# One kernel for clustered attention and two MoE layers: the planner of the MoE part may put rests and sums on GpSimd or VectorE, squares are formed without a rectified copy, and the last block's projections use other PSUM banks

## The chip, the core and the metric

The kernel runs on one core of a Trainium2 chip. TensorE multiplies matrices into PSUM, VectorE and ScalarE work on PSUM and SBUF, GpSimd on SBUF, and SyncE issues the DMAs. The metric is the device time of one execution in microseconds (us). A change is compared with the kernel before on the same chip.

## The reference

```python
def reference(**kwargs):
    attn_out = _attn_ref(**attn_kwargs)          # (2, 8, 768, 64): attention within 16 clusters
    x = attn_out.transpose(0, 2, 1, 3).reshape(B * S, H * D)      # 1536 tokens x 512
    x = _moe_ref(x=x, **moe_kwargs)
    return _moe2_ref(x=x, **moe2_kwargs)

def _moe_ref(x, w_gate, w_val, w_out, rms_g):    # 512 -> 1536 -> 512
    rms = np.sqrt(np.mean(x * x, axis=-1, keepdims=True) + 1e-06)
    xn = x / rms * rms_g
    g = xn @ w_gate
    silu = g * (1.0 / (1.0 + np.exp(-g)))
    return (silu * (xn @ w_val) @ w_out).astype(np.float32)

def _moe2_ref(x, w_in, w_out, s, b):             # 512 -> 2048 -> 512
    r = np.maximum(x @ w_in, 0.0)
    return ((s * (r * r) + b) @ w_out).astype(np.float32)
```

Inputs and outputs are float32 (some come as float64). The change touches the two MoE layers alone.

## The kernel before

Each operand of a matrix product is held as a high part (rounded to TensorE's fp32r format) and a low part, the **rest** (value minus high part). A product is three matmuls: high by high, high by rest, rest by high. So for each operand ScalarE writes the high part and GpSimd subtracts to get the rest: `split_h` (lines 1161 and 1164, tiles `gh` and `gl`) for the hidden values, `part_` (lines 1203 and 1205, tiles `xh`/`xl` and `eh`/`el`) for the inputs of the second layer, `split_w` and `add_pair` (tiles `wh`/`wl`) for the weights.

The 1536 tokens are four blocks `t` of 384 (`TB`), the 512 channels four chunks of 128. The first layer (`kind` 1) has 12 slices `f` of 128 hidden units, taken in pairs. For a slice and a block `unit1` makes gate and value products (12 matmuls each) in PSUM banks of the pool `ps_g` (tiles `pg`, tag "g", five banks); `proj` multiplies the hidden values of a pair with `w_out` and adds the result to `acc` in SBUF. Its products go to banks of the pool `ps_o` (tiles `po`, tag "o", three banks), and VectorE adds each to `acc`.

The second layer (`kind` 2) has 16 slices in eight pairs. `quad2` computes two slices for two blocks (blocks 2u and 2u+1) by seven block products instead of eight: products a, b, c, a again, d, e, d again, six matmuls each, joined by five additions on VectorE. That needs sums and differences of input blocks, the **forms** `t1` to `t4`, beside the blocks themselves (`11`, `21`, `22`), each split in high part and rest. `finish` then takes each of the four results through relu (ScalarE), square (VectorE, line 1343), scale and bias (ScalarE, line 1347) and `split_h`. The first product `a` is copied to SBUF by ScalarE (line 1334) before the same bank takes a further product.

The forms for u = 0 need the last result of the first layer (block 1 of its last pair of slices). `forms_last` makes them straight from the PSUM banks of that last projection: `proj` takes its chunks in the order 0, 2, 1, 3, VectorE adds the older sums to each in PSUM (line 1186), and after chunks 2 and 3 the form's differences follow (line 1280, and one on GpSimd, line 1293), each with high part and rest.

The order of instructions is not the order of the code. Each step is recorded with its engine, a duration, what it reads, what it writes and the buffers it takes; a planner, `Plan.run`, then sets them one by one in the queues of the engines. In the MoE part (`post`) the order on TensorE is that of the code (`strict`), and every other step has a due time from `due`, counted back from the TensorE step that needs it. The engine of each step is fixed. Each engine then runs its queue in order; a step that waits holds all behind it.

The main loop sets TensorE's order: after each `quad2` it calls `flush()`, which puts the projections that were held back:

```python
            else:
                if fs[0] == 0 and t != blocks[0]:
                    flush()
                quad2(fs, t, s)
                flush()
```

At the change of layers this gives: the quad u=1 of slices 0 and 1, the last projection of the first layer (block 1), the projections of blocks 2 and 3, the quad u=0, then the quad u=1 of slices 2 and 3.

Of the kernel before, what the change touches and what calls it, by code (L numbers as in the profile page):

```python
# [20 lines left out]
F32 = mybir.dt.float32  # L21
# [23 lines left out]
class Plan:  # L45
# [4 lines left out]
    def __init__(self, bufs, strict=()):  # L50
        self.ops, self.bufs, self.strict = [], bufs, strict
        self.last_w, self.readers, self.users = {}, {}, {}
# [30 lines left out]
    def due(self):  # L83


        ops, taken, after, t = self.ops, {}, {}, 0.0
        late = [1e9] * len(ops)
        for n, o in enumerate(ops):
            for d in {*o[3], *self.bufdeps(n, taken)}:
                if d != n:  # L90
                    after.setdefault(d, []).append(n)
            for tile in o[4]:
                taken.setdefault(tile[0], []).append(tile)
            if o[0] in self.strict:
                late[n], t = t, t + o[1]
        seen = set()

        def visit(n):
            if n not in seen:
                seen.add(n)  # L100
                for m in after.get(n, ()):
                    visit(m)
                    late[n] = min(late[n], late[m] - LATENCY[ops[n][0]] - ops[n][1] - 2.5 * bool(ops[n][6]))

        for n in range(len(ops) - 1, -1, -1):
            visit(n)
        self.ops = [(*o[:5], late[n], o[6]) for n, o in enumerate(ops)]

    def run(self):
        if self.strict:  # L110
            self.due()
# [10 lines left out]
        line = [n for n, o in enumerate(ops) if o[0] in self.strict][::-1]  # L122

        def start(n):
            if ops[n][0] in self.strict and n != line[-1]:
                return None
# [12 lines left out]
        while ready:  # L139
# [15 lines left out]
            if eng in self.strict:  # L155
                line.pop()
# [17 lines left out]

LATENCY = {"PE": .2, "ACT": .15, "DVE": .18, "POOL": .08, "SP": .65}
# [4 lines left out]
def attention_moe_moe2_kernel(  # L180
# [455 lines left out]
    def split_w(raw, to, j, ramp=None, at=None):  # L636
# [11 lines left out]
        stt(out=ui, in0=b, scalar=2.0 ** 31, in1=up_, op0=ALU.min, op1=ALU.subtract, reverse1=True)  # L648
        stt(out=ai, in0=low, scalar=5, in1=ui, op0=ALU.logical_shift_right, op1=ALU.bitwise_or)
# [340 lines left out]
    post = Plan({  # L990
# [3 lines left out]
    }, ("PE",))  # L994
# [10 lines left out]
    def then(eng, dur, fn, r, w, new=(), more=0.0):  # L1005
        add(eng, dur, fn, r=r, w=w, new=new, prio=now[0] + more)
# [443 lines left out]
```

## Time and profile before

| | us |
|---|---|
| median of 3 runs (811.73, 812.53, 816.11) | 812.53 |
| the profiled execution | 811.1 |
| span from its first to its last instruction | 809.4 |
| TensorE busy | 764.3 |
| VectorE, GpSimd, ScalarE busy | 572.0, 507.8, 483.2 |
| mean granted clock of TensorE, share of full | 0.992 |

The span is what the trace covers; the profiled time is 1.7 us more. The attention part takes the first 290 us or so: the first rest of the planned MoE part (line 1164) starts at 293.4 us. The products of the second layer start at 538.8 us and run to the end.

### The profile page before, as it was taken

What the parts mean: (1) busy time and instruction counts of PE and PEld (TensorE: products, weight loads), DVE (VectorE), ACT (ScalarE), POOL (GpSimd) and SP (SyncE); (2) the same over time, 40 slices, a digit from 0 to 9 for tenths busy, and PEclk for the clock granted to TensorE, in tenths of its full rate; (3) what the DMA queues carried; (4) which work ended last, traced back from release to release, by engine and by line L of the source; (5) the groups of instructions that cost most, each with busy time, mean ns of one, the idle gap of its engine ahead of it and who ended that gap; (6) DMA issues with size and microseconds to landing.
All of it is one profiled execution on the core that took longest, in us unless ns stands there. A gap on an engine that the chain in (4) does not pass through costs nothing.

```text
span 809.4 us, 14303 instructions
## 1 busy us (share of the span) xinstructions
PE 764.3 (94%) x5409; PEld 705.3 (87%) x5409; DVE 572.0 (71%) x933; ACT 483.2 (60%) x933; POOL 507.8 (63%) x464
## 2 busy tenths in 40 slices
PE   3899999799999899999999999997799999999998
PEld 1678877699998889999999999996788988998996
DVE  6898888988685767666646534446688788778855
ACT  5578789667758446555425333354676677667642
POOL 7599989968889335444423533698465664664632
PEclk9999999999999999999999999999899999999999
DMA  8476886254421014433311201100121212122004
GB/s 117 95 133 123 134 171 150 62 116 122 107 79 54 27 52 130 126 94 120 104 52 63 95 1 52 53 1 1 53 78 53 78 53 78 56 76 78 27 1 156
DMA packets 98821, 65.15 MB, mean 80 GB/s; under 512 B 64992, under 2 KB 89664, under 8 KB 98752
## 3 DMA queue, kind: packets, MB, share of 16 engines
q1 hardware_dynamic: 98752, 64.24, 31.6%
q8 instruction: 42, 0.69, 0.4%
q14 instruction: 27, 0.22, 0.1%
HBM read 48.45 MB, written 3.15 MB: 64 GB/s over the span
## 4 chain that ended last, share of the span: by engine, by line
PE 81%; DVE 10%; POOL 4%; ACT 3%; issue 2%; DMA 1%; DVEq 0%; POOLq 0%; ACTq 0%
PE pg L661 24%; PE po L675 16%; PE pg L1311 14%; PE po L673 10%; PE mps L450 4%; PE pv L521 3%; PE sps L481 3%; PE sps L482 2%; DVE mt L458 2%; POOL al L498 2%; PE pv L511 2%; PE pg L673 1%; DVE xn L575 1%; ACT a L487 1%; PE asps L397 1%
## 5 line engine op out<-in xcount | busy, mean ns | idle before, releaser
L1164 POOL TENSOR_TENSOR gl<-hv,gh 128x384 fp32r<-128x384 f32 x104 | 117.7, 1138 | 174.5 <-ACT gh L1161 174.4
L498 POOL TENSOR_TENSOR al<-a,ah 128x768 f16<-128x768 f32 x80 | 135.9, 1718 | 16.1 <-ACT ah L494 15.3
L661 PE MATMUL pg<-xh,wh 128*128 128x384 f32 x384 | 129.4, 337 | 2.5 <-DVE xl L591 1.4
L661 PE MATMUL pg<-xh,wl 128*128 128x384 f32 x384 | 128.5, 335 | 0.0
L661 PE MATMUL pg<-xl,wh 128*128 128x384 f32 x384 | 128.4, 334 | 0.0
L683 DVE TENSOR_TENSOR acc<-po,acc 128x512 f32<-128x512 f32 (+1 forms) x156 | 95.2, 624 | 41.9 <-PE po L673 21.7
L655 POOL TENSOR_TENSOR wl<-wa,wh 128x512 fp32r<-128x512 f32 x58 | 76.8, 1330 | 58.4 <-ACT wh L652 52.6
L487 ACT ACTIVATE a<-sps 128x384 f32<-128x384 f32 x192 | 86.0, 488 | 29.3 <-PE sps L482 27.4
L458 DVE TENSOR_REDUCE mt<-mps 128x1 fp32r<-128x768 f32 x96 | 90.1, 946 | 14.0 <-PE mps L450 13.0
L675 PE MATMUL po<-wh,gh 128*128 128x512 f32 x192 | 75.0, 391 | 0.6 <-DVE acc L683 0.6
L675 PE MATMUL po<-wh,gl 128*128 128x512 f32 x192 | 75.2, 392 | 0.0
L675 PE MATMUL po<-wl,gh 128*128 128x512 f32 x192 | 75.1, 391 | 0.0
L661 PEld LDWEIGHTS pg<-xh,wh 128*128 128x128 f32 x384 | 72.1, 188 | 3.5 <-DVE xl L591 1.7
L481 PE MATMUL sps<-q 128*128 128x384 f32 x192 | 70.5, 367 | 3.5 <-DMA q<-mT 1.2
L1161 ACT ACTIVATE gh<-hv 128x384 fp32r<-128x384 f32 x104 | 52.4, 516 | 33.8 <-DVE hv L1152 32.7
L661 PEld LDWEIGHTS pg<-xl,wh 128*128 128x128 f32 x384 | 72.1, 188 | 0.0
L661 PEld LDWEIGHTS pg<-xh,wl 128*128 128x128 f32 x384 | 72.1, 188 | 0.0
L482 PE MATMUL sps<-q 128*128 128x384 f32 x192 | 64.6, 337 | 0.0
L673 PE MATMUL po<-gh,wh 128*128 128x384 f32 x168 | 56.8, 338 | 5.5 <-DVE th L1280 4.5
L450 PE MATMUL mps<-q 127*128 127x384 f32 x192 | 56.3, 384 | 3.2 <-DVE mt L458 2.1
L673 PE MATMUL po<-gh,wl 128*128 128x384 f32 x168 | 56.5, 336 | 0.0
L673 PE MATMUL po<-gl,wh 128*128 128x384 f32 x168 | 56.5, 336 | 0.0
(187 smaller groups left out, 1985.3 us busy)
## 6 DMA issues: line engine op xcount, KB each, us to landing
raw<-in_moe_w_out_dram SPq DMA_DIRECT2D x30, 511.6 KB, 3.5
raw<-in_moe_w_in_dram SPq DMA_DIRECT2D x16, 510.5 KB
raw<-in_moe_w_gate_dram SPq DMA_DIRECT2D x14, 510.5 KB, 4.1
raw<-in_moe_w_val_dram SPq DMA_DIRECT2D x14, 510.5 KB, 4.2
q<-q SPq DMA_DIRECT2D x14, 384.0 KB
q<-q SPq DMA_DIRECT2D x28, 192.0 KB, 2.7
vr<-in_v_dram SPq DMA_DIRECT2D x8, 384.0 KB
out_dram<-acc SPq DMA_DIRECT2D x12, 256.0 KB, 2.0
```

Source lines behind the costliest of these rows:

```text
L450: nc.tensor.matmul(ps[:, e, 0:HALF], lhsT=x[0:127, 1, c * 128:c * 128 + 128], rhs=x[0:127, 2, e * HALF:(e + 1) * HALF], start=True, stop=T ...
L458: nc.vector.tensor_reduce(out=mt_of[i][:, c:c + 1], in_=m_t.pop((i, c))[:, :, 0:HALF], axis=AX.XY, op=ALU.max)
L481: nc.tensor.matmul(ps[:, 0:HALF], lhsT=x[:, 2, ks], rhs=x[:, 1, cs], start=True, stop=False)
L482: nc.tensor.matmul(ps[:, 0:HALF], lhsT=x[:, 3, ks], rhs=x[:, 0, cs], start=False, stop=True)
L487: act(out=a_t[i, c][:, e * HALF:(e + 1) * HALF], in_=s_t.pop((i, c, e))[:, 0:HALF], func=ACTF.Exp, scale=scale)
L498: nc.gpsimd.tensor_tensor(out=al, in0=a_t.pop((i, c)), in1=ah_t[i, c], op=ALU.subtract)
L661: nc.tensor.matmul(ps, lhsT=a[:, kk * 128:kk * 128 + 128], rhs=x[:, kk, :], start=(kk == m == 0), stop=(kk == KC - 1 and m == 2),)
L673: nc.tensor.matmul(ps, lhsT=a[:, cs], rhs=x, start=st[0], stop=st[1])
L675: nc.tensor.matmul(ps, lhsT=x[:, cs], rhs=a, start=st[0], stop=st[1])
L683: tt(out=ac, in0=ps, in1=ac, op=ALU.add)
L1164: gps(out=gl, in0=src(), in1=gh.bitcast(F32), op=ALU.subtract)
L1311: nc.tensor.matmul(B(x), lhsT=a[:, k_ * 128:k_ * 128 + 128], rhs=b[:, k_], start=(not more and k_ == m == 0), stop=(k_ == 1 and m == 2), s ...
```

## The change

The planner of the MoE part becomes a class of its own, `Post`. Some steps now have a second engine and a second duration (`alt`), and the planner gives a step to VectorE where it would end earlier there than on GpSimd by its own numbers. These are the rests `gl`, most rests of forms, some differences of forms, and the sums and rests of the weight pairs (`either`). The square of results `u2` and `u3` is one instruction that reads the value twice, `max(x, 0) * x`, without the relu on ScalarE ahead of it; that of `c22` keeps its relu and may be a multiplication on GpSimd; that of `c11` stays. The two integer steps on the weights are two steps of the planner instead of one. The last projection of the first layer takes its four banks from the "g" pool, and `forms_last` reads them there. In the first pair of slices of the second layer `flush(1)` holds one projection back (block 3), which then stands behind the quad u=0.

```diff
+class Post(Plan):
...
+    def run(self):
+        ops, late, xfer = self.ops, self.due(), 0.0
...
+                t = max([done[d] for d in (*deps, *old)], default=0.0)
+                at = max(t, free[eng])
+                by.setdefault(eng, []).append((at, late[n], n))
+                if n in self.alt:
+                    e2, d2 = self.alt[n]
+                    a2 = max(t, free[e2])
+                    if a2 + d2 + GAIN < at + dur:
+                        by.setdefault(e2, []).append((a2, late[n], n))
...
+GAIN = 0.0
...
-    post = Plan({
+    post = Post({
...
+    def either(dur, d2, fn, r, w, new=(), more=0.0):
+        post.alt[len(post.ops)] = ("DVE", d2)
+        add("POOL", dur, fn, r=r, w=w, new=new, prio=now[0] + more)
+
+    def two(eng):
+        return tt if eng == "DVE" else gps
...
-        add("DVE", 1.75, step, r=[raw, b], w=[key, ("wd", n)], prio=prio)
+        add("DVE", .72, step, r=[b], w=[key], prio=prio)
+        add("DVE", .97, step, r=[raw], w=[key, ("wd", n)], prio=prio)
...
-        def lo():
+        def lo(eng):
             gh, gl = hs_t[kind, f, t]
-            gps(out=gl, in0=src(), in1=gh.bitcast(F32), op=ALU.subtract)
+            two(eng)(out=gl, in0=src(), in1=gh.bitcast(F32), op=ALU.subtract)
         then("ACT", .52, hi, [key], [(*hg, "h")], [hg])
-        then("POOL", 1.04, lo, [key, (*hg, "h")], [(*hg, "l")])
+        either(1.08, .97, lo, [key, (*hg, "h")], [(*hg, "l")])
...
-            o = ("o", (kind, fs[0], t, c))
-            def mm(c=c, o=o):
-                new_bank(o, ps_o)
+            g_ = kind == 1 and last and t == last_t
+            o = ("g" if g_ else "o", (kind, fs[0], t, c))
+            def mm(c=c, o=o, at=None if g_ else ps_o):
+                new_bank(o, at)
...
+            def square2():
+                temp["th", n, u, x] = tp[p].tile([128, TB], F32, tag="th", name="th")
+                stt(out=temp["th", n, u, x], in0=src(), scalar=0.0, in1=src(), op0=ALU.max, op1=ALU.mult)
...
-            then("ACT", .5, relu, [sk], [tk], [tk])
-            then("DVE", .56, square, [sk], [tk])
+            if x == "c11":
+                then("ACT", .5, relu, [sk], [tk], [tk])
+                then("DVE", .56, square, [sk], [tk])
+            elif x in ON_POOL:
+                then("ACT", .5, relu, [sk], [tk], [tk])
+                either(1.08, .97, lambda eng: two(eng)(out=temp["th", n, u, x], in0=V(x), in1=temp["th", n, u, x], op=ALU.mult), [sk], [tk])
+            else:
+                then("DVE", .97, square2, [sk], [tk], [tk])
...
                 if fs[0] == 0 and t != blocks[0]:
-                    flush()
+                    flush(1)
                 quad2(fs, t, s)
                 flush()
```

By count of the instructions over the whole program: TensorE has the same matmuls; ScalarE loses 32 (the relus of `u2` and `u3`); GpSimd loses 46; VectorE gains 46, among them 31 rests `gl`, 12 rests of forms, 9 rests of weights and 4 differences, while 48 squares become 32 of the new form and 6 of the old (10 go to GpSimd).

On TensorE the first difference is at the last projection of the first layer. Its rows before, the first matmul of each group of six (`po_7479` to `po_7547` are its four chunks, `po_7560` and `po_7599` open the projections of blocks 2 and 3, `pg_7628` and `pg_7637` are products a and b of the quad u=0, `pg_7708` opens the next quad):

```order
L673 MATMUL po_7479<-gh_7374,wh2_6557 128x384
...
L673 MATMUL po_7547<-gh_7374,wh2_6557 128x384
...
L675 MATMUL po_7560<-wh2_7027,gh_7513 128x512
...
L675 MATMUL po_7599<-wh2_7027,gh_7523 128x512
...
L1311 MATMUL pg_7628<-xh0_7230,wh0_6806 128x384
...
L1311 MATMUL pg_7637<-eh0_7361,wh1_6824 128x384
...
L1311 MATMUL pg_7708<-xh2_6984,wh0_7304 128x384
```

The same place in the changed program (`pg_7501` to `pg_7536` are the four chunks, `po_7559` and `po_7689` open the projections of blocks 2 and 3, `pg_7606` and `pg_7627` are a and b, `pg_7732` opens the next quad):

```order
L740 MATMUL pg_7501<-gh_7376,wh2_6556 128x384
...
L740 MATMUL pg_7536<-gh_7376,wh2_6556 128x384
...
L742 MATMUL po_7559<-wh2_7027,gh_7494 128x512
...
L1395 MATMUL pg_7606<-xh0_7230,wh0_6806 128x384
...
L1395 MATMUL pg_7627<-eh0_7374,wh1_6824 128x384
...
L742 MATMUL po_7689<-wh2_7027,gh_7553 128x512
...
L1395 MATMUL pg_7732<-xh2_6984,wh0_7307 128x384
```

The chunks have other banks, and the 18 matmuls of block 3's projection stand behind the 42 of the quad instead of ahead of them. Nothing else on TensorE is moved.

On VectorE the rows of `forms_last` before (line 1186 adds the older sums, 1280 are differences of forms, 1205 rests, 681 the copies of the projections of blocks 2 and 3, 1329 the first addition of the quad u=0):

```order
L1186 TENSOR_TENSOR po<-po,acc_3778 128x384 x2
L1205 TENSOR_TENSOR xl_7360<-po,xh_7359 128x384
L1280 TENSOR_TENSOR th<-po,acc_3628 128x384
L1280 TENSOR_TENSOR hv<-po,th 128x384
L1280 TENSOR_TENSOR th<-po,th 128x384
L1280 TENSOR_TENSOR th<-po,acc_3628 128x384
L1186 TENSOR_TENSOR po<-po,acc_3778 128x384
L1280 TENSOR_TENSOR hv<-po,th 128x384
L1280 TENSOR_TENSOR th<-po,th 128x384
L1205 TENSOR_TENSOR xl_7360<-po,xh_7359 128x384
L681 COPY acc_7587<-po 128x512 x3
```

And in the changed program (1267 for 1186, 1364 for 1280, 1286 for 1205, 748 for 681, 1244 is a rest `gl`, 1377 the last difference):

```order
L1267 TENSOR_TENSOR pg<-pg,acc_3778 128x384 x4
L1244 TENSOR_TENSOR gl<-hv,gh 128x384
L1286 TENSOR_TENSOR xl_7373<-pg,xh_7372 128x384 x2
L748 COPY acc_7585<-po 128x512
L1364 TENSOR_TENSOR th<-pg,acc_3628 128x384 x2
L1364 TENSOR_TENSOR hv<-pg,th 128x384 x2
L1364 TENSOR_TENSOR th<-pg,th 128x384 x2
L1286 TENSOR_TENSOR el_7375<-hv,eh_7374 128x384
L1286 TENSOR_TENSOR el_7375<-th,eh_7374 128x384
L1377 TENSOR_TENSOR hv<-hv,acc_3628 128x384
L1286 TENSOR_TENSOR el_7375<-hv,eh_7374 128x384
```

The four additions now stand together ahead of all differences; one rest `gl`, three rests `el` and one difference have come to VectorE. In both programs the other `el` and the rests of `t1` are on GpSimd.

On ScalarE, the rows ahead of the copy of product a in the quad u=1 of slices 2 and 3, before (1340 relu, 1347 scale and bias, 1161 high part, 652 high part of a weight, 1334 the copy):

```order
L1161 ACTIVATE gh_7738<-hv_7719 128x384
L1340 ACTIVATE th_7746<-hv_7644 128x384
L1347 ACTIVATE hv_7668<-th_7717,b_col_82,s_col_80 128x384
L1347 ACTIVATE hv_7690<-th_7706,b_col_82,s_col_80 128x384
L1347 ACTIVATE hv_7644<-th_7746,b_col_82,s_col_80 128x384
L1161 ACTIVATE gh_7754<-hv_7668 128x384
L1161 ACTIVATE gh_7757<-hv_7644 128x384
L1161 ACTIVATE gh_7761<-hv_7690 128x384
L652 ACTIVATE wh2_7764<-wa1_7692 128x512
L1334 ACTIVATE hv_7768<-pg_7708 128x384
```

And in the changed program (1434 scale and bias, 1241 high part, 1418 the copy, 719 high part of a weight):

```order
L1434 ACTIVATE hv_7685<-th_7661,b_col_82,s_col_80 128x384
L1241 ACTIVATE gh_7696<-hv_7685 128x384
L1434 ACTIVATE hv_7673<-th_7682,b_col_82,s_col_80 128x384
L1241 ACTIVATE gh_7711<-hv_7673 128x384
L1434 ACTIVATE hv_7663<-th_7702,b_col_82,s_col_80 128x384
L1241 ACTIVATE gh_7727<-hv_7663 128x384
L1434 ACTIVATE hv_7624<-th_7714,b_col_82,s_col_80 128x384
L1241 ACTIVATE gh_7739<-hv_7624 128x384
L1418 ACTIVATE hv_7760<-pg_7732 128x384
L719 ACTIVATE wh2_7769<-wa1_7508 128x512
```

The relus of `u2` and `u3` are gone, and the high part of the weight has moved behind the copy.

## Rows read from the trace of the kernel before

**Rows 1.** First part of the page: busy time, share of the span, instructions
```profile
PE 764.3 (94%) x5409; PEld 705.3 (87%) x5409; DVE 572.0 (71%) x933; ACT 483.2 (60%) x933; POOL 507.8 (63%) x464
```

**Rows 2.** TensorE's waits from 380 us on: count and longest in us
```profile
PE po L673 <- DVE th L1280: 4.5, 1, 4.5
PE pg L1311 <- ACT hv L1334: 4.4, 1, 4.4
PE po L675 <- DVE acc L683: 0.6, 1, 0.6
```

**Rows 3.** Busy time by stretch; last three columns granted clock, DMA share, GB/s
```profile
375.00:546.08 171.08, 171.08 (x988) 170.96 (x987) 87.67 (x147) 70.34 (x130) 83.46 (x78) 1.00 0.18 56
546.08:586.14 40.06, 31.13 (x146) 28.92 (x145) 25.77 (x41) 23.63 (x47) 27.03 (x26) 0.87 0.09 27
586.14:804.00 217.86, 217.25 (x1080) 194.81 (x1080) 166.72 (x257) 140.30 (x260) 123.85 (x116) 1.00 0.20 65
```

**Rows 4.** Timeline of TensorE: start, duration, instruction, wait ahead of it
```profile
546.08 0.33 PE L673 MATMUL po<-gh,wh 128*128 128x384 f32 x1
...
549.03 0.34 PE L673 MATMUL po<-gh,wl 128*128 128x384 f32 x1
553.85 0.69 PE L673 MATMUL po<-gh,wh 128*128 128x384 f32 x1 [4.48 <-DVE th L1280]
...
564.68 0.33 PE L1311 MATMUL pg<-xh,wh 128*128 128x384 f32 x1
...
574.94 0.34 PE L1311 MATMUL pg<-eh,wl 128*128 128x384 f32 x1
579.73 0.69 PE L1311 MATMUL pg<-xh,wh 128*128 128x384 f32 x1 [4.45 <-ACT hv L1334]
...
586.14 0.39 PE L675 MATMUL po<-wh,gh 128*128 128x512 f32 x1
...
594.34 0.33 PE L1311 MATMUL pg<-xh,wh 128*128 128x384 f32 x1
```

**Rows 5.** Stretches around two idles of TensorE, columns as in rows 3
```profile
158.00:160.20 2.20, 0.07 (x1) 0.01 (x1) 2.18 (x3) 1.36 (x5) 2.20 (x4) 1.00 0.54 128
161.10:164.60 3.50, 3.46 (x42) 3.39 (x43) 2.82 (x6) 0.00 (x0) 1.36 (x1) 0.51 1.04 183
553.85:557.16 3.31, 3.31 (x9) 3.07 (x10) 2.05 (x4) 2.34 (x6) 3.31 (x4) 0.51 0.00 0
```

**Rows 6.** Line 1343 (squares): duration ns as minimum, median, maximum; first, last start
```profile
L1343 DVE SCALAR_TENSOR_TENSOR th<-hv,th x48: 541/551/2641, 545.7 to 791.4; 128x384 f32<-128x384 f32 x48
```

**Rows 7.** Timeline of VectorE, columns as in rows 4
```profile
545.71 2.64 DVE L1343 SCALAR_TENSOR_TENSOR th<-hv,th 128x384 f32<-128x384 f32 x1
...
549.21 0.55 DVE L1186 TENSOR_TENSOR po<-po,acc 128x384 f32<-128x384 f32 x1
549.68 0.54 DVE L1343 SCALAR_TENSOR_TENSOR th<-hv,th 128x384 f32<-128x384 f32 x1
...
558.77 1.37 DVE L681 COPY acc<-po 128x512 f32<-128x512 f32 x2
...
573.42 3.39 DVE L1343 SCALAR_TENSOR_TENSOR th<-hv,th 128x384 f32<-128x384 f32 x3
```

**Rows 8.** Timeline of ScalarE
```profile
551.03 1.34 ACT L1161 ACTIVATE gh<-hv 128x384 fp32r<-128x384 f32 x3
...
552.64 0.85 ACT L1284 ACTIVATE th<-po 128x384 f32<-128x384 f32 x2
...
575.57 0.71 ACT L1347 ACTIVATE hv<-th,b_col,s_col 128x384 f32<-128x384 f32 x1 [0.76 <-DVE th L1343]
...
579.21 0.47 ACT L1334 ACTIVATE hv<-pg 128x384 f32<-128x384 f32 x1
```

**Rows 9.** Timeline of GpSimd
```profile
543.98 3.96 POOL L1205 TENSOR_TENSOR xl<-acc,xh 128x384 fp32r<-128x384 f32 x4
```

**Rows 10.** VectorE's waits between 586 and 804 us
```profile
DVE acc L683 <- PE po L675: 18.6, 36, 0.7
```

More of the change, by code (lines that the diff above doesn't have):

```diff
@@ L81, in bufdeps @@
         return deps
[L83 to L107, printed above, removed]
     def run(self):
-        if self.strict:
-            self.due()
         ops, self.xfer = self.ops, 0.0
@@ L1120, in add_pair @@
             add("ACT", .63 if n > 256 else .42, call(hi_, i, j, n), r=[src], w=[(*tile, "h")], new=[tile], prio=prio)
-            add("POOL", 1.31 if n > 256 else .67, call(lo_, i, j, n), r=[src, (*tile, "h")], w=[(*tile, "l")], prio=prio)
+            either(1.35 if n > 256 else .8, 1.2 if n > 256 else .7, lambda eng, i=i, j=j, n=n: lo_(i, j, n, eng), [src, (*tile, "h")], [(*tile, "l")])
+    ON_POOL = ("c22",)
     FORM = {"11": (0, 0), "12": (0, 0), "s1": (1, 1), "s2": (1, 1), "s3": (2, 0), "22": (2, 0), "s4": (3, 1)}
@@ L1203, in hi, with lo @@
             act(out=to()[0], in_=src(), func=ACTF.Copy)
-        def lo():
-            (gps if eng == "POOL" else tt)(out=to()[1], in0=src(), in1=to()[0].bitcast(F32), op=ALU.subtract)
+        def lo(e=eng):
+            two(e)(out=to()[1], in0=src(), in1=to()[0].bitcast(F32), op=ALU.subtract)
         then("ACT", .52, hi, [sk], [ks[0]], more=more)
-        then(eng, 1.04 if eng == "POOL" else .56, lo, [sk, ks[0]], [ks[1]], more=more)
+        if eng == "POOL":
+            either(1.08, .97, lo, [sk, ks[0]], [ks[1]], more=more)
+        else:
+            then(eng, .56, lo, [sk, ks[0]], [ks[1]], more=more)
     def chunk(t, c):
@@ L1249, in forms_, with sub @@
             ):
-                def sub(i=i, a=a, b=b, k_=k_, take=take):
+                def sub(eng, i=i, a=a, b=b, k_=k_, take=take):
                     if i == 0:
                         take()
-                    gps(out=temp["t", t, k_][i], in0=a(), in1=b(), op=ALU.subtract)
-                then("POOL", 1.04, sub, r, [tk[i]], tk if i == 0 else (), more=4)
+                    two(eng)(out=temp["t", t, k_][i], in0=a(), in1=b(), op=ALU.subtract)
+                either(1.08, .97, sub, r, [tk[i]], tk if i == 0 else (), more=4)
                 part_(T[i], tk[i], at_form(u, name, k_), ks[name], more=4)
@@ L1292, in forms_last @@
         part_(T[0], tk[0], at_form(u, "t1", k_), ks["t1"])
-        then("POOL", 1.04, lambda: gps(out=T[3](), in0=T[1](), in1=y[m](), op=ALU.subtract), [tk[1], (*ac0, m)], [tk[3]])
+        either(1.08, .97, lambda eng: two(eng)(out=T[3](), in0=T[1](), in1=y[m](), op=ALU.subtract), [tk[1], (*ac0, m)], [tk[3]])
         part_(T[3], tk[3], at_form(u, "t4", k_), ks["t4"])
```

116 lines of the change are left out of this document (96 added, 20 removed).

## Prediction

> **What bounds the kernel now.** I read the busy times first, then TensorE's waits, then the stretch around the waits instruction by instruction. TensorE is busy for 764.3 us, 94% of the span [rows 1], and the change removes no matmul. So it can gain only where TensorE waits or runs slowly. In the planned MoE part TensorE is full from 375 to 546 us and, but for 0.6 us, from 586 to 804 us [rows 3]. The stretch between is 40.06 us long and holds both long waits: 4.48 us ahead of the fourth chunk of the last projection, 4.45 us inside the quad u=1 of slices 2 and 3 [rows 2, 4]. It is also the one stretch whose clock is below full (0.87).
>
> What would it take without waits? Matmuls of 384 columns follow each other every 0.1735 us (17 steps from 546.08 to 549.03), those of 512 columns every 0.228 us (36 steps from 586.14 to 594.34) [rows 4]. It holds 24 + 84 of the first and 36 of the second: 18.7 + 8.2 = 26.9 us. So 13.1 us are lost: 8.9 of waits, the rest in matmuls at half clock behind them. After the first wait the granted clock was 0.51 for 3.31 us, that is the 1.2 GHz level [rows 5]; nine matmuls took 3.31 us instead of 6 x 0.1735 + 3 x 0.228 = 1.7 us, a loss of 1.6 us. 13.1 us is the ceiling of any gain.
>
> **Why it waits.** The fourth chunk needs one of three "o" banks, which is free only when VectorE's difference of line 1280 and ScalarE's copies at 552.64 have read the first chunk [rows 8]. VectorE was late: a square that takes 0.55 us alone lasted 2.64 us from 545.71 [rows 6, 7], while GpSimd ran four rests back to back until 547.94 [rows 9]. The second wait is for ScalarE's copy of product a at 579.21 [rows 8]. It stands behind the scales, which waited for three squares that took 3.39 us together [rows 7, 8].
>
> **The change, part by part.**
>
> *Other banks.* The four chunks find banks of the quad before them; by the changed order these are last read by additions and a square that VectorE runs by about 546. The last of them, the subtraction for e, stood ahead of the square of 545.71 before [rows 7]; even 2 us late it is done ahead of the fourth chunk at 546.08 + 18 x 0.1735 = 549.2. So the first wait goes from this place. The four chunks end at 546.08 + 24 x 0.1735 = 550.24.
>
> *The held-back projection.* Block 2's 18 matmuls follow until 550.24 + 18 x 0.228 = 554.34. Then the quad u=0 starts, where before two projections stood. Product a needs old forms only; product b needs the new form t2, its rest from the second matmul on, at 554.34 + 1.04 + 0.17 = 555.55. This is what is late next. VectorE makes that rest. After the last chunk's matmul has ended (550.07 + 0.33) its queue holds four instructions of 384 columns, a copy, six differences and the rest of t2. Instructions of 384 columns follow every 0.47 us, a copy takes 0.68 [rows 7]: 10 x 0.47 + 0.68 + 0.55 = 5.93, so 556.4 at the earliest. Two of them, the rest `gl` and the rest of t2, read two tiles in SBUF as the late square did and run beside GpSimd's rests. Nothing shows this operation on VectorE before; the nearest row is the square of the same size: 0.55 alone, 2.64 at worst [rows 6]. Held for nothing, both give 556.4; held as the worst square, 556.4 + 2 x 2.1 = 560.6. GpSimd's instructions take 0.99 us [rows 9]; I take one whole such hold for the first, which stands among GpSimd's own rests, and half a one for the second: 557.9. So TensorE waits 2.35 us there (bounds 0.85 and 5.05). The first rest of u3 is due at the fifth matmul of block 2's projection, at 551.15; ScalarE's three scales and high parts (a step of 0.45 [rows 8]) and one rest of GpSimd behind the delayed squares put it near 551.4: 0.3 us more (bounds 0 and 1).
>
> *Clock.* An idle of 2.15 us at 158 us was followed by 3.5 us at 0.51 [rows 5]. A wait of 2.35 us is like it, so I add 1.6 us (bounds 0 and 1.6; at 0.85 us no row shows a fall).
>
> *The second wait.* Block 3's projection now lies between the quads, 4.10 us. Before, the earlier quad ended at 564.68 + 42 x 0.1735 = 571.97, the copy at 579.21 + 0.47: 7.7 us later. Ahead of the copy two relus and two high parts of weights are gone, at a step of 0.45 each [rows 8] 1.8 us, so about 5.9 us. TensorE now needs it 4.10 + 3 x 1.04 = 7.2 us after that quad's end. So this wait of 4.45 and its slow stretch go, with 1.3 us to spare.
>
> *Rests, sums and squares on other engines, elsewhere.* TensorE does not wait outside that stretch, so nothing can be gained. The cover: VectorE is busy 167 of 218 us after 586, and of its idle time 18.6 us is waiting for TensorE in 36 additions [rows 3, 10]. By the changed order a pair of slices there has two more instructions on VectorE: four single squares for six, 2.2 rests `gl`, one weight rest, 0.8 products for `c22` less the two squares it had. That is 1 to 2 us in a pair's 31. GpSimd does 0.99 us less for each that moves. Splitting the integer step changes only where its halves may stand, over the same instructions. Cost zero; without the cover it is the slower rival below.
>
> **The sum.** Of 13.1 us lost, 2.35 + 0.3 + 1.6 = 4.25 come back, so the gain is 8.9 us. The profiled execution took 811.1 with a span of 809.4, and becomes 802.2. The median of the runs is 812.5, 1.4 above it; against that the forecast is 803.6. About 0.5%, or 4 us, is what a measurement of this kernel tells from no change.
>
> **A rule that speaks against it.** Rows 6 show that a VectorE instruction with two SBUF inputs takes 0.54 to 2.64 us for the same work. The Trainium skill, "SBUF — State Buffer", section "Who interferes with whom", says that such an instruction contends with a GpSimd instruction that reads SBUF, and that whoever starts first blocks the other wholly. The 2.64 us beside four GpSimd rests agrees, and is more than one blocked instruction would give. By that rule moved rests buy no overlap with GpSimd; what it would make of the time is the slower rival.
>
> **The rivals.**
>
> *Both stalls go and nothing comes back*: 812.5 - 13.1 = 799.4. It needs the rest of t2 by 555.6, 0.8 us ahead of what VectorE's queue can do unhindered; for it speaks only that a quad already under way hides part of the wait.
>
> *The first stall moves whole*: if the two rests are held as the worst square was, TensorE waits 5 us at product b and the slow stretch follows, so only the second is gained: 13.1 - 5.05 - 1.6 - 0.3 = 6.2, and 806.3.
>
> *The second stall returns*: if the squares of the quad u=0 are held as the three at 573.42 were and more, the copy is later than 7.2 us. From 1.3 us of extra hold on each microsecond is lost, up to the 13.1 - 4.48 - 1.6 = 7.0 us that this wait and its slow matmuls cost before. Then the gain is 2 to 4.5: 808 to 810.5, mostly no measurable change. Against it: the 1.3 us to spare and fewer ScalarE instructions.
>
> *Slower: VectorE's additions of the projections fall behind.* Three "o" banks and 1.37 us (6 x 0.228) per product leave VectorE about 2.7 us; an addition takes 0.68. If a rest or square between them is held 2.1 us, TensorE waits some tenths. There are 14 such runs of projections after 586; at 0.65 us in each (8.9 / 14) the gain is gone, at 1 us the time is 803.6 + 14 = 817.6. For it speaks the 0.6 us wait of this kind already there [rows 2]. Against it: in the changed order a pair has seven instructions with two SBUF inputs between the first and last addition of its two runs, and it had seven before, with GpSimd busier.
>
> **How the numbers follow.** Forecast (801.5 to 805.5) 0.55; nothing comes back 0.10; first stall whole 0.17; second returns 0.11; slower 0.07. The range 799.2 to 808.0 holds the first three, 0.82. Faster by over 0.5% means below 808.4: 0.82 and a little of the fourth, 0.83; within 0.5% 0.10; slower 0.07.
>
> **What will show it.** Right: no wait of TensorE at the last projection (line 740); one of 1 to 3 us at the second or third product of the quad u=0, released by a rest on VectorE, with a half-clock stretch of some 3.4 us; none at the copy of line 1418; the stretch from the last projection to the third pair's first projection near 31 us instead of 40.06; nothing from then to the end. Wrong: TensorE waiting for additions of line 750 all through the second layer (the slower rival), a wait of 4 us or more for line 1418, or a first wait that stays at line 740.

## The result

The changed kernel took 804.77 us (median of six runs, 803.46 to 807.27), the kernel before 812.13 us (median of six, 810.42 to 816.11). The ratio is 0.9912 with a 95% interval of 0.9884 to 0.9940: faster by 7.4 us, where 8.9 us were forecast (803.6). The range of 799.2 to 808.0 holds it.

The profiled execution of the changed kernel took 807.27 us, the longest of its six. Its first matmul of the first layer comes at 157.88 us, before at 154.93; what happens ahead of that lies outside the change and differs from run to run. So stretches are compared here, not ends. The first row is the page's first part; the others are the windows view of the changed kernel (columns as in [rows 3]): ahead of the first quad, from there to the first projection of the third pair of products (the change of layers), and on to the last matmul.

```profile
PE 765.4 (95%) x5409; PEld 704.2 (87%) x5409; DVE 616.2 (76%) x979; ACT 470.4 (58%) x901; POOL 461.3 (57%) x418
```

```profile
375.00:541.30 166.30, 166.30 (x961) 166.30 (x960) 106.47 (x170) 70.44 (x128) 60.77 (x54) 1.00 0.19 61
541.30:547.70 6.40, 6.40 (x37) 6.09 (x36) 4.55 (x9) 3.29 (x7) 6.40 (x6) 1.00 0.01 1
547.70:579.98 32.28, 29.53 (x152) 26.52 (x151) 29.62 (x47) 22.21 (x43) 19.22 (x18) 1.00 0.11 33
579.98:801.55 221.57, 219.40 (x1086) 195.91 (x1086) 180.31 (x272) 128.68 (x232) 107.31 (x102) 1.00 0.20 65
```

VectorE has 44 us more to do than in [rows 1], GpSimd 46.5 us less. The clock is full in these four stretches, where [rows 3] have 0.87 at the change of layers. Three sums make the result:

| stretch, us | before | after | gain |
|---|---|---|---|
| change of layers: 538.80 to 586.14, now 541.30 to 579.98 | 47.3 | 38.7 | 8.7 |
| second layer from there to the last matmul (805.38, now 801.55) | 219.2 | 221.6 | -2.3 |
| one wait at 361.8 us | 1.1 | 0 | 1.1 |

The three come to 7.4 us, as much as the medians differ; that the two meet so closely is chance, since the interval of the ratio is 2.3 us wide to either side. TensorE's waits after, beside [rows 2] (the same view, from 280 us; count and longest):

```profile
PE pg L1395 <- DVE hv L1413: 3.5, 8, 0.8
...
PE pg L1395 <- DVE el L1286: 1.1, 1, 1.1
...
PE pg L1395 <- ACT eh L1284: 0.2, 1, 0.2
```

The two long waits of [rows 2] are gone. What took their place at the change of layers is seen in TensorE's timeline (columns as in [rows 4]):

```profile
547.37 0.34 PE L1395 MATMUL pg<-eh,wl 128*128 128x384 f32 x1
548.48 0.45 PE L1395 MATMUL pg<-xh,wh 128*128 128x384 f32 x1 [0.77 <-DVE hv L1413]
...
549.63 0.33 PE L740 MATMUL pg<-gh,wh 128*128 128x384 f32 x1
...
557.92 0.33 PE L1395 MATMUL pg<-xh,wh 128*128 128x384 f32 x1
...
558.80 0.34 PE L1395 MATMUL pg<-xh,wl 128*128 128x384 f32 x1
559.39 0.44 PE L1395 MATMUL pg<-eh,wh 128*128 128x384 f32 x1 [0.24 <-ACT eh L1284]
560.93 0.44 PE L1395 MATMUL pg<-el,wh 128*128 128x384 f32 x1 [1.10 <-DVE el L1286]
...
567.39 0.44 PE L1395 MATMUL pg<-xh,wh 128*128 128x384 f32 x1 [0.55 <-DVE hv L1413]
...
575.82 0.33 PE L1395 MATMUL pg<-xh,wh 128*128 128x384 f32 x1
...
579.98 0.39 PE L742 MATMUL po<-wh,gh 128*128 128x512 f32 x1
```

From 549.63 (last projection, line 740) to 557.92 (product a of the quad u=0) nothing waits: 8.29 us, by the forecast 24 x 0.1735 + 18 x 0.228 = 8.27. Product b waits for the rest `el` on VectorE, as forecast. The copy of product a (line 1418) is not waited for. Not forecast are the waits for a join (line 1413) at 548.48 and 567.39, and six more like it in the second layer, at 610.1 us and then every 31.7 us to 768.4 us. The first and the last of these:

```profile
609.78 0.34 PE L1395 MATMUL pg<-eh,wl 128*128 128x384 f32 x1
610.48 0.44 PE L1395 MATMUL pg<-xh,wh 128*128 128x384 f32 x1 [0.36 <-DVE hv L1413]
...
768.06 0.34 PE L1395 MATMUL pg<-eh,wl 128*128 128x384 f32 x1
768.76 0.45 PE L1395 MATMUL pg<-xh,wh 128*128 128x384 f32 x1 [0.36 <-DVE hv L1413]
```

In the pitch of the matmuls each costs 610.48 - 609.78 - 0.17 = 0.53 us, and the matmuls just behind it follow a little more slowly: the quad that holds the first one takes 611.63 - 603.68 = 7.95 us, the quad before it, without a wait, 595.48 - 588.18 = 7.30. So each costs 0.65 us, six 3.9 us. The second layer is only 2.3 us longer because the kernel before loses 1.6 us there which are gone now: 0.9 at its wait of 0.6 us [rows 2], the rest in four small gaps inside quads. VectorE's timeline there, and below it GpSimd's, show what the join stands behind:

```profile
607.09 0.56 DVE L1413 TENSOR_TENSOR hv<-pg,hv 128x384 f32<-128x384 f32 x1 [0.47 <-PE pg L1395]
607.56 1.67 DVE L713 SCALAR_TENSOR_TENSOR wa<-wb,wa 128x512 int32<-128x512 f32 x1
609.26 0.69 DVE L716 SCALAR_TENSOR_TENSOR wa<-raw,wa 128x512 int32<-128x512 int32 x1
609.87 0.55 DVE L1413 TENSOR_TENSOR hv<-pg,hv 128x384 f32<-128x384 f32 x1
```

```profile
607.38 1.30 POOL L722 TENSOR_TENSOR wl<-wa,wh 128x512 fp32r<-128x512 f32 x1 [5.29 <-ACT wh L719]
```

The first integer step takes 1.67 us, the second 0.69. GpSimd's rest of a weight began 0.18 us ahead of the first and lasted 1.30 us. That the one holds the other is an inference so far; experiment 12 decides it.

### The profile page after: what moved, and what is told of

Read it like the earlier page. It is cut to its first block, busy times and chain, and to the rows that moved or that the text cites. A ratio compares the mean times of both kernels' runs of the same rounds, so it can differ in the third digit from the quotient of the medians.

```text
span 805.5 us, 14231 instructions
## 1 busy us (share of the span) xinstructions
PE 765.4 (95%) x5409; PEld 704.2 (87%) x5409; DVE 616.2 (76%) x979; ACT 470.4 (58%) x901; POOL 461.3 (57%) x418
## 4 chain that ended last, share of the span: by engine, by line
PE 77%; DVE 10%; POOL 7%; issue 3%; ACT 2%; DMA 1%; SPq 0%; DVEq 0%; POOLq 0%; ACTq 0%
PE pg L728 23%; PE po L742 16%; PE pg L1395 11%; PE po L740 9%; PE mps L515 4%; PE pv L586 3%; PE sps L546 3%; POOL al L563 3%; PE sps L547 2%; DVE mt L523 2%; PE pv L576 2%; PE pg L740 2%; DVE wa L713 1%; POOL ah L557 1%; DVE xn L640 1%
## 5 line engine op out<-in xcount | busy, mean ns | idle before, releaser
L1244 POOL TENSOR_TENSOR gl<-hv,gh 128x384 fp32r<-128x384 f32 x73 | 82.5, 1135 | 119.5 <-ACT gh L1241 119.5
L750 DVE TENSOR_TENSOR acc<-po,acc 128x512 f32<-128x512 f32 (+1 forms) x156 | 97.1, 625 | 37.7 <-PE po L742 19.3
L523 DVE TENSOR_REDUCE mt<-mps 128x1 fp32r<-128x768 f32 x96 | 90.2, 947 | 13.8 <-PE mps L515 12.7
L713 DVE SCALAR_TENSOR_TENSOR wa<-wb,wa 128x512 int32<-128x512 f32 x52 | 53.2, 1023 | 18.9 <-ACT wb L711 13.3
L719 ACT ACTIVATE wh<-wa 128x512 fp32r<-128x512 f32 x58 | 36.3, 628 | 35.6 <-DVE wa L716 29.1
L586 PEld LDWEIGHTS <-ah 128*128 128x128 f16 x960 | 47.3, 98 | 7.0 <-issue 5.9
```

Source lines behind the costliest of these rows:

```text
L523: nc.vector.tensor_reduce(out=mt_of[i][:, c:c + 1], in_=m_t.pop((i, c))[:, :, 0:HALF], axis=AX.XY, op=ALU.max)
L750: tt(out=ac, in0=ps, in1=ac, op=ALU.add)
L1244: two(eng)(out=gl, in0=src(), in1=gh.bitcast(F32), op=ALU.subtract)
```

## The experiments

All are changes of the changed kernel but 5, 10 and 11, which are parts of the change put into the kernel before. "Change" is the stretch at the change of layers (38.7 us after, 47.3 before), "steady" the rest to the last matmul (221.6 and 219.2). Without a wait the change would take 34.2 us: 42 matmuls of the first quad by 0.1735 us, 7.3, and the 26.9 us that the prediction worked out.

**1. Without the projection held back.**

```diff
-                    flush(1)
+                    flush()
```

> All of the change but the projection held back: block 3's projection stands ahead of the quad u=0 again. My theory (the held-back projection is what covers the copy of product a): TensorE's wait of 2.0 us around product b of the quad u=0 shrinks to under 0.5, since the quad starts 4.1 us later, and a wait for the copy of line 1418 comes back at the next quad: the copy is ready some 5.4 us after the earlier quad's end and needed 3.1 us after it, so 2 to 3 us, with a half-clock stretch behind it possible (1.6). Against the changed kernel between 0 and 3 us slower, near 806. The rival, that ScalarE without the relus is fast enough by itself and the order does not matter: no wait for line 1418, 1.5 to 2 us faster than the changed kernel.

803.64 us, ratio 0.9887 (0.9857 to 0.9918); change 41.1, steady 217.7. The timeline of TensorE has no wait at product b, and the second wait of before is back, with the half clock behind it (matmuls of 0.52 us from 575.58 on):

```profile
569.88 0.34 PE L1395 MATMUL pg<-eh,wl 128*128 128x384 f32 x1
574.05 0.44 PE L1395 MATMUL pg<-xh,wh 128*128 128x384 f32 x1 [3.83 <-ACT hv L1418]
...
575.58 0.52 PE L1395 MATMUL pg<-xh,wl 128*128 128x384 f32 x1
```

So the projection held back is what hides the copy, and what makes product b wait. The squares without a rectified copy, which this kernel has, do not remove that wait. As a whole the kernel is not slower than the changed one, which had been expected: it loses 2.5 us at the change of layers and gains 3.8 behind it, where it has none of the six waits.

**2. With the old banks.**

```diff
-            g_ = kind == 1 and last and t == last_t
+            g_ = False
...
-        ok = [("g", (1, last_pair[0], t, c)) for c in (k_, m)]
+        ok = [("o", (1, last_pair[0], t, c)) for c in (k_, m)]
```

> All of the change but the other banks: the last projection uses the three banks of the pool for projections again. My theory (the banks took away the wait ahead of the fourth chunk): TensorE waits 3 to 5 us there again, with the clock at half behind it, and the forms come later by as much; 4 to 6 us slower than the changed kernel, 809 to 811. The rival, that VectorE's relief alone brings the forms in time: a wait under 1.5 us there and no more than 1.5 us slower.

805.58 us, 0.9908 (0.9877 to 0.9940); change 41.3, steady 219.7. The first wait is back at its old place, the fourth chunk of the last projection:

```profile
546.99 0.34 PE L740 MATMUL po<-gh,wl 128*128 128x384 f32 x1
551.99 0.69 PE L740 MATMUL po<-gh,wh 128*128 128x384 f32 x1 [4.67 <-DVE th L1364]
```

So the banks remove this wait, and nothing else in the change does. The time is below the 809 to 811 us that were expected: the second layer has three of the six waits.

**3. The integer steps one planner step again.**

```diff
-        add("DVE", .72, step, r=[b], w=[key], prio=prio)
-        add("DVE", .97, step, r=[raw], w=[key, ("wd", n)], prio=prio)
+        add("DVE", 1.75, step, r=[raw, b], w=[key, ("wd", n)], prio=prio)
```

> All of the change, but the two integer steps on the weights are one step of the planner again. The changed kernel has six new waits of 0.36 us in the second layer, each at the second part of product d, for a join that stands behind an integer step which GpSimd held. My theory (the split lets the planner set such a step between two joins): those six waits go or shrink, TensorE's time from the third pair's first projection to the end falls by 1.5 to 2.4 us, and the time is 802 to 804. The rival (the rests and squares moved to VectorE make them): as many waits as in the changed kernel, 804 to 806.

801.82 us, 0.9866 (0.9832 to 0.9900); change 38.7, steady 218.1. The six waits are gone. Taken by itself this says that the split costs 3 us; experiments 8, 10 and 11 show that it is not the split as such: they have the steps whole, and the same waits. Every edit of a step makes the planner set the whole order anew.

**4. Nothing placed on VectorE by the planner.**

```diff
-GAIN = 0.0
+GAIN = 1e9
```

> All of the change but the choice of engine: the planner never takes VectorE for a step of two engines, so all these rests, sums and the squares of c22 are GpSimd's. My theory: the banks and the held-back projection bring most; without VectorE's rests GpSimd makes the ten rests of the forms one after the other, so the rest of t2 is 1 to 3 us later and TensorE waits 3 to 5 us at product b of the quad u=0 instead of 2.0, with the clock at half behind it; the steady part is free of the six waits. Together 0 to 4 us slower than the changed kernel, 805 to 809. The rival (the placement makes the gain): 809 or more. A second rival (the placement is only a burden): faster than the changed kernel by 1 us or more.

805.97 us, 0.9912 (0.9881 to 0.9944); change 43.0, steady 218.0. TensorE's waits:

```profile
PE pg L1395 <- ACT hv L1418: 2.5, 2, 1.6
PE pg L1395 <- DVE hv L1413: 1.6, 1, 1.6
PE pg L1395 <- POOL el L1286: 1.5, 5, 0.7
```

Without the placement the change of layers is 4.3 us longer: in the quad u=0 product b waits for rests on GpSimd, and in the next quad the copy and a join are late. In the second layer this kernel has no wait, so that its time is that of the changed kernel, within the noise: by the whole, the placement is not shown to bring anything.

**5. The two edits of TensorE's order alone, in the kernel before**: the other banks (with their keys in `forms_last`), and the projection held back.

```diff
-            o = ("o", (kind, fs[0], t, c))
+            g_ = kind == 1 and last and t == last_t
+            o = ("g" if g_ else "o", (kind, fs[0], t, c))
...
-                    flush()
+                    flush(1)
```

> The kernel before with two edits alone: the four banks of the last projection from the other pool, and the projection held back. Planner, engines and squares stay. My theory: the steady part is as before (219.2 us from the third pair's first projection to the last matmul, 219 expected), and the change of layers takes about as long as with the engine choice off, 43 us, instead of 47.3 before and 38.7 in the changed kernel. Time 806.5 to 809. The rival (these two edits bring nothing without the new planner): 811 or more; a second rival (they bring all): 805 or less.

805.65 us (twelve runs, 804.34 to 815.14), 0.9953 (0.9921 to 0.9984); change 40.9, steady 219.2. They give 6.4 of the 8.7 us, with no clock below full in that stretch. Product b waits 1.62 us for a rest `el`, a later product 0.99 us for a rest `xl`, both on GpSimd. Here the wait at 361.8 us is still there, as in 10 and 11; it is gone in each kernel with the new planner. From the first quad to the last matmul this kernel takes 799.93 - 539.78 = 260.2 us, the changed kernel 801.55 - 541.30 = 260.3, the kernel before 266.6. So these two edits bring what is gained there; all the rest of the change (planner, placement, squares, split) gains 2.2 us at the change of layers, loses 2.3 behind it, and takes away the wait at 361.8 us. The intervals of the two kernels' ratios overlap.

**6. VectorE's planner prefers the step that is due first, within 0.8 us.**

```diff
-                lim = min(c)[0] + P["look"][ENGINES.index(eng)]
+                lim = min(c)[0] + (0.8 if eng == "DVE" else P["look"][ENGINES.index(eng)])
```

**7. The same on top of 3.**

> The changed kernel with one number of its planner: on VectorE it looks 0.8 us ahead instead of 0.11 for a step that is due earlier, so that a join just out of reach is put ahead of an integer step. The integer step stays split. My theory (the six waits, and the one of 0.77 us in the first quad, come from an integer step set in just ahead of a join): they go, the part from the third pair on takes 217.7 to 218.5 instead of 221.6 us, the change of layers is some 0.5 to 1 us shorter; 800 to 803. The rival (the split itself, or the load of VectorE, makes them): as many waits as in the changed kernel, 803 to 806.

> One integer step again, and the planner's look ahead of 0.8 us on VectorE. If the order ahead of joins is the only cost, the steady part stays at 218.0 and the wait of 1.48 us in the first quad of the second layer goes: 800 to 801.5, 1 us faster than with the single integer step alone. If waiting for joins delays other steps: slower than that, 802 to 804.

6: 803.35 us, 0.9900 (0.9887 to 0.9914); change 35.3, steady 223.8. 7: 810.29 us, 0.9975 (0.9961 to 0.9989); change 35.0, steady 230.8. Both nearly empty the change of layers of waits and are slower behind it: against the changed kernel, run 6 gains 3.4 us and loses 2.3, against experiment 3, run 7 gains 3.7 us and loses 12.7. In 6 the six waits for a join are gone, as expected, and none of the first integer steps in the second layer takes 0.8 us or more. Six waits of 0.31 us came in their place, at the second turn of product a. They are for ScalarE's copy (line 1418), which stands behind a high part there (TensorE's and ScalarE's timelines):

```profile
601.27 0.45 PE L1395 MATMUL pg<-xh,wh 128*128 128x384 f32 x1 [0.32 <-ACT hv L1418]
```

```profile
600.31 0.53 ACT L1241 ACTIVATE gh<-hv 128x384 fp32r<-128x384 f32 x1
600.74 0.47 ACT L1418 ACTIVATE hv<-pg 128x384 f32<-128x384 f32 x1
```

So the planner's choice does remove the waits for joins, and brings others. 7 has six waits of 1.05 us for the same copy (line 1414 there) and six of 0.40 us at projections, for VectorE's additions and copies. Why ScalarE and VectorE are late there was not followed further.

**8. The old squares on top of 3** (relu on ScalarE and square on VectorE for all four results).

```diff
-            if x == "c11":
...
+            then("ACT", .5, relu, [sk], [tk], [tk])
+            then("DVE", .56, square, [sk], [tk])
```

> One integer step, and all squares as before (relu on ScalarE, square on VectorE), the rest of the change kept. My theory (the squares bring little: the copy of product a had 1.3 us to spare, and TensorE has no other wait for ScalarE): within 1 us of the kernel with the single integer step and the new squares, 801 to 803, steady part 218 to 219. The rival (the new squares free ScalarE in time for the copy): a wait for the copy of product a at the third quad, 2 us or more slower.

807.42 us, 0.9952 (0.9940 to 0.9965); change 41.1, steady 221.0. The change takes 2.4 us more than in 3: waits of 1.45 us in the first quad (3 has one of 1.48 there too), 1.74 us at product b, 1.54 us at 577.5 us. None is for the copy. So the kernel with the old squares is slower there; whether by the squares or by the other order that goes with them is not separated. In the second layer five waits of 0.36 us are back, behind an integer step of 1.67 us beside a weight's rest on GpSimd, though the steps are not split.

**9. The preference of 6 for the early part alone, on top of 3.**

```diff
+                lim = min(c)[0] + (0.8 if eng == "DVE" and len(line) > 210 else P["look"][ENGINES.index(eng)])
```

> One integer step, and the look ahead of 0.8 us on VectorE only until the third quad or so; after it 0.11 as in the change. My theory (joins first is right at the change of layers, where TensorE waits for them, and wrong after it, where it delays the additions of the projections): the change of layers takes 35 to 36.5 us as with the look ahead everywhere, the steady part 218 as with the single integer step; 798 to 800.5, faster than every kernel so far. If the two parts are not independent: 801 or more.

799.77 us, 0.9852 (0.9829 to 0.9875); change 36.2, steady 218.7. This computes all of it and beats the kernel before by 12.7 us and the changed kernel by 5.0. The bound of 210 steps was chosen for this one order; it shows what the order holds, no rule for another.

**10 and 11. Each edit of TensorE's order alone, in the kernel before**: the banks (10), `flush(1)` (11), as in the diff of 5.

> The kernel before with the four banks of the last projection from the other pool as the only edit. My theory (each stall has a cause of its own): the wait ahead of the fourth chunk goes with its half-clock stretch, the one for the copy of product a stays near 4.4 us; the change of layers takes about 41 us instead of 47.3; 806 to 807. The rival (the gain of the two edits together is that of the banks alone, or of none): 805.5, or over 810.

> The kernel before with the projection held back as the only edit. My theory: the wait of 4.5 us ahead of the fourth chunk stays, the one for the copy goes, and product b of the quad u=0 now waits for the rest of t2, 3 us or more, as the forms are as late as before and the quad starts 4.1 us earlier; the change of layers takes 42 to 45 us; 807 to 810. The rival (holding back alone brings the whole gain): 41 us, 805.5.

10: 808.78 us, 0.9956 (0.9940 to 0.9972); change 43.6, steady 221.2; the copy is waited for 3.42 us, with half clock behind it, and four waits of 0.17 to 1.05 us for high parts and rests in the quad u=0 had not been expected. 11: 810.68 us, 0.9972 (0.9956 to 0.9988); change 43.9, steady 222.4; the fourth chunk waits 4.48 us as before. The wait at product b that was expected for 11 did not come: its quad u=0 starts 14.5 us after the last projection's first matmul, where it starts 8.3 us after it in the changed kernel, late enough for the forms. A wait of 1.86 us for a join in the next quad came instead. Each takes 3.5 to 3.7 us off the change of layers by removing its own wait, as 1 and 2 have it from the other side, and each brings five or six waits of 0.36 us. Without the split, the new squares or any placed rest, this is VectorE's timeline of 11 at the first of them, and GpSimd's:

```profile
611.71 1.73 DVE L648 SCALAR_TENSOR_TENSOR wa<-wb,wa 128x512 int32<-128x512 f32 x1
613.47 0.69 DVE L649 SCALAR_TENSOR_TENSOR wa<-raw,wa 128x512 int32<-128x512 int32 x1
614.07 0.55 DVE L1329 TENSOR_TENSOR hv<-pg,hv 128x384 f32<-128x384 f32 x1
```

```profile
611.59 1.29 POOL L655 TENSOR_TENSOR wl<-wa,wh 128x512 fp32r<-128x512 f32 x1 [3.46 <-ACT wh L652]
```

**12. The same order, without GpSimd's read beside the integer step.**

```diff
-        nc.gpsimd.tensor_tensor(out=l, in0=a, in1=h.bitcast(F32), op=ALU.subtract)
+        if fine and j == 2:
+            nc.gpsimd.memset(l.bitcast(F32), 0.0)
+        else:
+            nc.gpsimd.tensor_tensor(out=l, in0=a, in1=h.bitcast(F32), op=ALU.subtract)
```

> The changed kernel with one instruction exchanged: in the planned part GpSimd no longer reads the weights for the rests of w_out, but only writes zeros in their place (these rests are left out of the computation); the order on VectorE stays as it was. Theory: the first integer step ahead of the six late joins takes 1.67 us because GpSimd reads SBUF for such a rest while VectorE reads its two inputs there. Then this step takes about 0.7 us, the six waits of 0.36 us at the second part of product d go, the steady part falls from 221.6 to between 218 and 219.5 us, and the time comes to 802 to 803.5 us. Rival: the waits come from the place of the integer steps ahead of the join alone, or from ScalarE's late inputs. Then the waits stay at 0.3 to 0.4 us each, the steady part at 221 to 222 us, and the time at 804 to 806 us.

This kernel leaves the rests of the planned part's `w_out` weights out of the computation. 800.52 us, 0.9859 (0.9833 to 0.9886); change 38.7, steady 217.8. VectorE's instructions stand in the order of the changed kernel; this is the same place (this run is 4.0 us ahead):

```profile
603.59 0.68 DVE L713 SCALAR_TENSOR_TENSOR wa<-wb,wa 128x512 int32<-128x512 f32 x1
604.30 0.69 DVE L716 SCALAR_TENSOR_TENSOR wa<-raw,wa 128x512 int32<-128x512 int32 x1
605.14 0.56 DVE L1416 TENSOR_TENSOR hv<-pg,hv 128x384 f32<-128x384 f32 x1
```

The integer step takes 0.68 us for 1.67, the join is in time, and all six waits are gone, while those at the change of layers are as in the changed kernel. The rival, that the place of the steps in the order is enough, has fallen: the place is the same. It takes both, the place just ahead of the join and GpSimd's rest beside the step. The other runs agree. In the second layer after, 2, 8, 10 and 11 have six, three, five, five and six of these first integer steps of 1.65 us or more, and as many waits for joins. 4 has five of 1.55 or 1.56 us beside such a rest, each ahead of an addition of a projection and not of a pair's second step and a join, and no wait. 1, 3 and 9 have none of 1.5 us or more and none of the six waits. That it is GpSimd's read and not merely its being at work isn't separated: the zeros don't wait for the weight, were written 5 us earlier (at 598.52), and nothing ran on GpSimd beside the step. The steady part came out a little below the 218 us that the theory gave, the time below its 802 to 803.5.

## Why the prediction was right, and where not

**The first wait goes with the banks.** Right: no wait at line 740 after, 4.67 us there in experiment 2.

**The second wait goes with the projection held back.** Right, 3.83 us back in 1. The forecast put the copy's end 5.9 us after the earlier quad's, 1.3 us ahead of need. It came at 574.49, 5.94 us after that quad's last matmul had made room (568.55), and 1.33 us ahead of the matmul at 575.82. The reason given for the 5.9 us was wrong in part, and that the number came out is luck: ScalarE was idle for 0.57 us ahead of the copy and waited for product a itself, so it was done with its other work earlier than forecast, and TensorE's own order set the copy's time. The lead came from the 4.10 us of the projection, and the relus taken away were not what decided: 1 has the new squares and waits 3.83 us, 8 and 11 have the old ones with the projection held back and wait for the copy 0 and 0.17 us.

**Product b waits for the rest of t2.** Right in place and engine. Set against the projection's first matmul, the rest was forecast to end 557.9 - 546.08 = 11.8 us later and ended at 560.88, 11.25 us later. The two holds beside GpSimd that it priced at 1.5 us came to 1.1: the rest `gl` at 554.46 us took 1.39 us and the rest of t2 at 560.10 us 0.78, where 0.54 is undisturbed. The quad's waits at product b sum to 0.42 + 1.37 + 0.25 + 0.13 = 2.2 us in the pitch, by the forecast 2.35 (0.85 to 5.05). The 0.3 us for the first rest of u3 did not occur.

**The clock, 1.6 us.** Wrong: no half clock followed. The wait came in pieces, the longest 1.10 us, with matmuls between, where the row it was taken from [rows 5] has one idle of 2.15 us. Of the waits in the experiments that of 1.86 us in 11 was followed by matmuls at the 1.2 GHz level, and those of 1.74 us in 8 and 1.62 us in 5 were not. The length of a wait does not settle it: TensorE has a wait of 1.4 us near 290 us in both kernels, behind the same last twenty matmuls, and only in the profiled execution of the changed kernel half clock followed (0.57 granted from 290 to 294 us; 1.00 before). TensorE's timeline there:

```profile
290.03 0.44 PE L728 MATMUL pg<-xh,wh 128*128 128x384 f32 x1 [1.41 <-DVE xl L656]
...
290.80 0.52 PE L728 MATMUL pg<-xh,wh 128*128 128x384 f32 x1
```

Why it fell in one and not in the other is open, so 1.6 us or nothing could not be told from these rows.

**The sum at the change of layers.** 8.7 us gained, 8.9 forecast. The agreement is partly luck: in place of the 1.6 and 0.3 us that did not occur, two waits for joins came that were not foreseen, 0.94 us in the first quad and 0.72 us in the quad u=0. The first has its row in VectorE's timeline:

```profile
546.80 0.69 DVE L713 SCALAR_TENSOR_TENSOR wa<-wb,wa 128x512 int32<-128x512 f32 x1 [1.52 <-ACT wb L711]
547.41 0.55 DVE L1427 SCALAR_TENSOR_TENSOR th<-pg,th 128x384 f32<-128x384 f32 x1
547.88 0.54 DVE L1413 TENSOR_TENSOR hv<-pg,hv 128x384 f32<-128x384 f32 x1
```

An integer step set ahead of the join waited 1.52 us for ScalarE. The stretch that the prediction named, from the last projection to the third pair's first one, was forecast near 31 us and took 579.98 - 549.63 = 30.35.

**"Rests, sums and squares on other engines, elsewhere ... Cost zero".** This step failed, with 3.9 us lost at six waits for joins (2.3 net of the 1.6 us that the kernel before lost there). Its cover was VectorE's idle time, a sum over a pair's 31 us. That time was there; it did not help, because a join is due within tenths of a microsecond, and one step held for 1 us just ahead of it is late whatever VectorE does later. The mechanism was the one of the slower rival, an instruction held beside GpSimd in front of one that TensorE waits for. The rival looked for it at the additions of the projections (line 750), and counted instructions there; it stood at the joins. And it is not the placement as such that brought it: 4 has none of the six waits, neither have 1 and 3, while 10 and 11 have them without any placed rest.

**"TensorE does not wait outside that stretch, so nothing can be gained".** Wrong by 1.6 us behind that stretch, where [rows 2] had a wait of 0.6 us and the kernel after has it no more, and by 1.1 us ahead of it, since TensorE's waits were read from 380 us on. The kernel before has one at 361.8 us, ahead of a chunk of a projection, and VectorE's timeline shows the same pair of integer steps ahead of the addition that frees its bank:

```profile
359.20 1.66 DVE L648 SCALAR_TENSOR_TENSOR wa<-wb,wa 128x512 int32<-128x512 f32 x1
360.89 1.39 DVE L649 SCALAR_TENSOR_TENSOR wa<-raw,wa 128x512 int32<-128x512 int32 x1
362.20 1.47 DVE L683 TENSOR_TENSOR acc<-po,acc 128x384 f32<-128x384 f32 x3
```

GpSimd runs a weight's rest of 1.29 us from 359.02 and another rest of 1.46 from 360.27 there. So this loss and the six of after look alike, though no experiment took this one apart. The order after has no such place at 362 us, and six of them later. Why the planner makes one order or the other was not followed.

**What stays open.** Why the copy comes late in 6 and 7; how much of the 2.4 us in 8 is the squares and how much another order; and when a wait of 1.4 to 1.9 us is followed by half clock.

## What to carry to other kernels

Read TensorE's waits over the whole planned part before a term is set to zero, and ask of each engine not only how much idle time it has but what stands just ahead of the instructions that TensorE needs within a few tenths of a microsecond. Where a planner sets the order, an edit's cost cannot be told from taking that edit out, since that gives another order: here three kernels without the split had the waits that "the split" seemed to cause, and only an edit that kept the order showed the cause. Repair the few late steps at one place of the order, as experiment 9 did; as a rule for the whole program the same preference gave back 2.3 of 3.4 us in 6, and 12.7 for 3.7 in 7. And put the simple parts of a change into the old kernel alone (5) before the rest is given credit: here two edits of TensorE's order bring nearly all of the gain.

## What the runs showed of the hardware

A VectorE instruction with two inputs in SBUF was held by a single GpSimd rest for about 1 us (0.68 us in experiment 12, 1.67 to 1.73 us beside a rest of 1.29 or 1.30 us). Where both engines have several such instructions, they run interleaved and both are slower. VectorE's and GpSimd's timelines of the changed kernel, behind product b:

```profile
560.80 1.36 DVE L1286 TENSOR_TENSOR el<-th,eh 128x384 fp32r<-128x384 f32 x1
562.08 1.37 DVE L1377 TENSOR_TENSOR hv<-hv,acc 128x384 f32<-128x384 f32 x1
563.38 1.37 DVE L1286 TENSOR_TENSOR el<-hv,eh 128x384 fp32r<-128x384 f32 x1
```

```profile
559.45 1.01 POOL L1377 TENSOR_TENSOR hv<-hv,acc 128x384 f32<-128x384 f32 x1
560.42 1.33 POOL L1286 TENSOR_TENSOR el<-hv,eh 128x384 fp32r<-128x384 f32 x1
561.71 1.33 POOL L1286 TENSOR_TENSOR el<-th,eh 128x384 fp32r<-128x384 f32 x1
```

One of each is done every 1.29 us (560.42 to 561.71), where an undisturbed VectorE starts one every 0.47 us [rows 7] and GpSimd one every 0.99 [rows 9]. The Trainium skill, "SBUF — State Buffer", section "Who interferes with whom", says that a VectorE instruction with two SBUF inputs contends with a GpSimd instruction that reads SBUF, that the ports they share are an exclusive lock, and that issue order decides who blocks. The integer step agrees: GpSimd's rest ends at 607.38 + 1.30 = 608.68, and the step 0.55 us after that. For a row of such instructions, two by turns without any overlap would need 0.47 + 0.99 = 1.46 us (an estimate from the rows named); the trace has 1.29, and GpSimd alone would take 1.98. So a moved rest does buy time here, 0.69 us a pair, and by this estimate 0.17 of it is overlap, which the prediction had denied by this rule. What that is worth alone no run shows: experiment 4, 4.3 us longer at the change of layers, also has another order.
